# Attention output written token by token, softmax scale moved behind the AV product, chunks transposed at load: a fused attention and two-MoE kernel on one core

## The chip, the cores and the metric

The kernel runs on one core of a Trainium2 chip. The time is device microseconds of one execution; the time before is the median of three runs. Engines are named as in the profile: PE is TensorE (PEld its weight loads), DVE is VectorE, ACT is ScalarE, POOL is GpSimd, and SP is the queue that issues most DMAs.

## The reference

Three layers follow each other. The inputs are drawn at random; all arithmetic is float32.

```python
# attention: B, H, S, D = 8, 8, 576, 64; keys and values are averaged in groups of 8
k_p = k.reshape(B, H, S // 8, 8, D).mean(axis=3)           # 72 keys per head
v_p = v.reshape(B, H, S // 8, 8, D).mean(axis=3)
scores = (1 / np.sqrt(D)) * (q @ k_p^T)
attn = np.exp(scores - max(scores)); attn /= attn.sum(-1, keepdims=True) + 1e-09
x = (attn @ v_p).transpose(0, 2, 1, 3).reshape(4608, 512)   # tokens x (heads, d)
# first MoE (dense): d_model 512, d_ff 1536
g = x @ w_gate
x = (g * sigmoid(g) * (x @ w_val)) @ w_out
# second MoE: 8 experts, top 1, d_ff 1024
logits = x @ w_gate2 + modality_bias[modality_id]; e = argmax(logits)
out = softmax(logits)[e] * (relu(x @ w1[e]) @ w2[e])
```

## The kernel before

**Attention.** The 4608 tokens are worked through in 36 steps of 128 tokens. Two batches make a group of nine steps: a batch has 576 tokens, so four full steps each, and one step (`i == 4`) that takes the last 64 tokens of both. For each batch k is averaged on DVE (`k_pool`, `kp`) and v on POOL (`v_pool`, three adds in a row on `vraw`), and `v_finish` spreads the averaged v into a block-diagonal tile `vb` on POOL. A step runs: `st_scores` (PE writes `sc`, DVE takes the maximum `nm`, ACT makes eight exponentials `e`, one for each head); `st_norm` (DVE sums to `sm`, POOL adds 1e-9, DVE takes the reciprocal, POOL multiplies `e` by it); `st_aT` (PE transposes `e` into `aTp`, DVE or ACT copies it to `at`). `st_av` then works on 256 or 320 tokens at once, for two heads at a time: PE multiplies with `vb` as the stationary operand, so that `xp` has features on partitions and tokens along the row, ACT copies it to `xs`, and the result goes to DRAM already transposed (`xT_d`).

**First MoE.** The tokens are taken in 12 chunks of 384. `x_load` brings a transposed chunk from `xT_d` in four pieces (`xr`) and splits each into a high and a low part (`xh` on ACT, `xl` on DVE) that PE multiplies in its faster float32 form. `gemm1` does 24 matmuls `gv` per chunk and slice of d_ff, `gemm2` nine matmuls `x`. Chunks 0 and 1 run interleaved, because the weights are still being split (`w_split`) then. `x_load(c + 2)` is called after the last `gemm1` of chunk c; `x_load(0)` and `x_load(1)` are called inside the attention. PSUM has eight banks: two of tag `s`, four of tag `x`, two of tag `y`. The output of `gemm2` holds one `y` bank as long as a chunk runs.

**Second MoE.** Routing, then 19 blocks of 256 gathered tokens; `x_trans` transposes each gathered tile on PE (`tp`), and ACT and DVE split it.

**Order.** The attention's pieces are called in the order of keys given by hand (`at_key(x, fn, ...)`, sorted). The build reorders instructions from there and writes one list for each engine; an engine works through its list strictly in order, and so does the SP queue with its DMAs. Where an instruction waits, everything behind it on that engine waits as well.

Of the kernel before, what the change touches and what calls it, by code (L numbers as in the profile page):

```python
# [21 lines left out]
POOL = 8  # L22
# [16 lines left out]

CONST_W = [  # L40
    ("ident", 128), ("vmask", 16), ("idhi", TILES), ("idlo", TILES), ("iota", 128), ("keyw", E), ("le8", E * E),
# [3 lines left out]
def const_array():  # L45
    import numpy as np

    p = np.arange(128)
    parts = {"ident": np.eye(128)}
    vm = np.zeros((128, 4, 2, 2))  # L50
    for r in range(H * KEYS):
        c, row, h = r // 128, r % 128, r // KEYS
        vm[row, h // 2, c - h // 2, h % 2] = 1.0 / 8
    parts["vmask"] = vm.reshape(128, 16)
# [12 lines left out]
def attention_moe_moe2(ctx: ExitStack, tc: tile.TileContext, q, k, v, w_gate, w_val, w_out,  # L67
# [13 lines left out]
    xT_d = [dram.tile([128, 4, 2 * S], F32, name=f"xT{g}") for g in range(4)]  # L81
# [22 lines left out]
    NW1 = 2  # L104
# [71 lines left out]
    def x_load(c):  # L176
        src = xT_d[c // 3]
        c0 = (c % 3) * CH
        hi, lo = [], []
        for k2 in range(2):  # L180
            th = m1.tile([128, 2, CH], F32R, tag="xh", bufs=4, name="xh")
            tl = m1.tile([128, 2, CH], F32R, tag="xl", bufs=4, name="xl")
            for j in range(2):
                raw = m1.tile([128, CH], F32, tag="xr", bufs=2, name="xr")
                sy.dma_start(out=raw, in_=src[:, 2 * k2 + j, c0:c0 + CH])
                ac.copy(th[:, j, :], raw)
                ve.tensor_tensor(out=tl[:, j, :], in0=raw, in1=th[:, j, :].bitcast(F32), op=ALU.subtract)
                hi.append(th[:, j, :])
                lo.append(tl[:, j, :])
        xc[c] = (hi, lo)  # L190
# [3 lines left out]
    with tc.tile_pool(name="p0", bufs=1) as p0:  # L194
# [3 lines left out]
        e_t = [p0.tile([128, 640], F32, name=f"e{i}") for i in range(NE)]  # L198
# [3 lines left out]
        for t in e_t:  # L202
            gp.memset(t[:, 576:640], 0.0)

        k_raw, v_raw, vb_t, q_t, at_t, xs_t, nm_t, sm_t = {}, {}, {}, {}, {}, {}, {}, {}
# [5 lines left out]
        def k_load(b):  # L211
            k_raw[b] = p0.tile([128, 4 * KEYS, POOL], F32, tag="kraw", bufs=2, name="kraw")
            sy.dma_start(out=k_raw[b].rearrange("p k r -> p (k r)"), in_=k[b])

        def v_load(b):
            v_raw[b] = p0.tile([128, 5, POOL, 64], F32, tag="vraw", bufs=2, name="vraw")
            sy.dma_start(out=v_raw[b].rearrange("p c r d -> p (c r d)"), in_=v[b])

        def k_pool(b):
            raw = k_raw.pop(b)  # L220
            kp = p0.tile([128, 4 * KEYS], F32, tag="kp", bufs=2, name="kp")
            ve.tensor_reduce(out=kp, in_=raw, op=ALU.add, axis=AX.X)  # L222
            for w in range(2):
                ps = slice(64 * w, 64 * w + 64)
                ac.activation(out=kb_t[b % 2][ps, :, w, :], in_=kp[ps].rearrange("p (a k) -> p a k", a=4),
                              func=ACTF.Copy, scale=1.0 / 64)

        def v_pool(b):
            t = v_raw.pop(b)
            for w in (4, 2, 1):  # L230
                o = t[:, :, 0:w] if w > 1 else vs_t[b % 2].unsqueeze(2)
                gp.tensor_tensor(out=o, in0=t[:, :, 0:w], in1=t[:, :, w:2 * w], op=ALU.add)  # L232

        def v_finish(b):
            vb = p0.tile([128, 4, 2, 2, 64], F32, tag="vb", bufs=2, name="vb")
            vm = C_["vmask"].rearrange("p (a w r) -> p a w r", a=4, w=2)
            for w in range(2):
                gp.tensor_tensor(out=vb[:, :, w], in0=vs_t[b % 2][:, w:w + 4, :].unsqueeze(2)  # L238
                                 .to_broadcast([128, 4, 2, 64]),
                                 in1=vm[:, :, w].unsqueeze(3).to_broadcast([128, 4, 2, 64]), op=ALU.mult)  # L240
            vb_t[b] = vb.rearrange("p a w r d -> p a w (r d)")
# [36 lines left out]
        def at_tile(b, half):  # L278
            if (b, half) not in at_t:
                at_t[b, half] = p0.tile([128, 5, 256 + 64 * half], F32, tag=f"at{half}", bufs=2, name=f"at{half}")  # L280
            return at_t[b, half]

        def st_aT(x):
            b, i = steps[x]
            e = e_t[x % NE]
            if i < 4:
                views = [(b, i // 2, slice(0, 128), slice(i % 2 * 128, i % 2 * 128 + 128))]
            else:
                views = [(b + w, 1, slice(64 * w, 64 * w + 64), slice(256, 320)) for w in range(2)]
            for c0, cn in ((0, 4), (4, 1)):  # L290
                ap = bank("y", "aTp")[:, 0:cn * 128].rearrange("p (c n) -> p c n", c=cn)
                for c in range(cn):
                    pe.transpose(ap[:, c, :], e[:, (c0 + c) * 128:(c0 + c + 1) * 128], ident)
                for bb, half, ss, cs in views:
                    o = at_tile(bb, half)[:, c0:c0 + cn, cs]
                    if cn == 1 or x % 2:
                        ve.tensor_copy(o, ap[:, :, ss])  # L297
                    else:
                        ac.copy(o, ap[:, :, ss])

        def st_av(b, half, hp):
            n = 256 + 64 * half
            if hp == 0:
                xs_t[b, half] = p0.tile([128, 4, 320], F32, tag="xs", bufs=2, name="xs")
            xs = xs_t[b, half]
            xp = bank("s", "xp")
            for w in range(2):
# [12 lines left out]
        as_, an, av, avs = 3.0, 1.7, 0.7, 0.45  # L320
# [4 lines left out]
        for g in range(4):  # L325
            for b in (2 * g, 2 * g + 1):
                x = 9 * g + (4 if b % 2 else 0) - as_ - 1.0
                at_key(x, k_pool, b)
                at_key(x - 4.0, k_load, b)
                at_key(x - 3.9, q_load, b)  # L330
                x0 = 9 * g + (6 if b % 2 else 1) + av
                at_key(x0 - 1.5, v_finish, b)
                at_key(x0 - 3.0, v_pool, b)
                at_key(x0 - 5.5, v_load, b)
                x1 = 9 * g + (8 if b % 2 else 4) + av
                for hp in range(4):
                    at_key(x0 + hp * avs, st_av, b, 0, hp)
                    at_key(x1 + hp * avs, st_av, b, 1, hp)
        for n in range(3 * NW1 + 4):
            if n < 4:  # L340
                at_key(12.0 + n, w_load, n)
            else:
                at_key(21.0 + (n - 4) * 2.5 + 0.1, w_load, n)
        for n in range(3 * NW1):
            at_key(21.0 + n * 2.5, w_split, n)
        at_key(5.0, load_bias, p0)
# [479 lines left out]
```

## Time and profile before

| | before |
|---|---|
| time, median of 3 runs | 1577.84 us (1576.95 to 1580.01) |
| the profiled execution's own time | 1575.83 us |
| its span in the trace | 1574.1 us |
| first matmul `gv` of the first MoE starts | 192.3 us |
| PE busy, share of the span | 1505.1 us, 96% |
| DVE / ACT / POOL busy | 949.3 / 617.1 / 194.5 us |
| mean granted TensorE clock | 0.983 |

The span runs from the first to the last instruction. A busy share is an average over stages that have different limits: up to 192.3 us no engine is busy all the time, and from there to the end of the first MoE PE is.

### The profile page before, as it was taken

To read this page: it belongs to the slowest core of one execution; us is meant where nothing else is said; L and a number is where in the kernel's file an instruction comes from. 1 tells how busy PE (TensorE), PEld (TensorE's weight loads), DVE (VectorE), ACT (ScalarE), POOL (GpSimd) and SP (SyncE) were. 2 spreads that over 40 slices of the span, in tenths; PEclk is the share of its full clock that TensorE was granted. 3 is DMA by queue.
4 is the path that set the end of the run, shared out by engine and by line. 5 is a ranking of instruction groups with operands and counts; after the bars stand their busy time and mean duration, and the time that the engine had idled before them with its cause. 6 is when DMAs were issued, how large, how long until landed. Compare 5 with 4: busy or idle time off the path is not lost.

```text
span 1574.1 us, 22647 instructions
## 1 busy us (share of the span) xinstructions
PE 1505.1 (96%) x8472; PEld 1367.7 (87%) x8472; DVE 949.3 (60%) x2252; ACT 617.1 (39%) x1385; POOL 194.5 (12%) x201
## 2 busy tenths in 40 slices
PE   5778899999999999999999999999999999999996
PEld 4566699999999999999999999998889889898985
DVE  5677799555555564637272727277986666666660
ACT  4567555432222121212121212123556656666661
POOL 4866300000000000000000000001031111211101
PEclk8998999999999999999999999999999999999998
DMA  7775534210000000000010100007477666666520
GB/s 287 291 268 187 184 139 161 67 31 30 11 30 31 11 31 31 11 30 24 17 41 1 40 1 31 1 21 265 141 231 258 224 229 223 218 225 224 191 98 28
DMA packets 47816, 179.58 MB, mean 114 GB/s; under 512 B 5421, under 2 KB 19921, under 8 KB 34898
## 3 DMA queue, kind: packets, MB, share of 16 engines
q1 hardware_dynamic: 33170, 149.19, 26.9%
q0 software_dynamic: 6080, 19.42, 3.5%
q10 hardware_dynamic: 8448, 9.44, 1.7%
q8 instruction: 68, 1.11, 0.3%
q14 instruction: 50, 0.41, 0.1%
HBM read 149.70 MB, written 28.86 MB: 113 GB/s over the span
## 4 chain that ended last, share of the span: by engine, by line
PE 85%; DVE 4%; issue 4%; POOL 4%; DMA 2%; ACT 1%; POOLq 0%; SPq 0%; ACTq 0%
PE gv L372 38%; PE x L394 19%; PE hp L665 12%; PE po L684 12%; PE xp L308 2%; POOL vraw L232 1%; PE tp L649 1%; POOL e L276 1%; DVE kp L222 1%; DMA x2d<-row 1%; ACT e L267 1%; DVE sm L273 1%; DVE at L297 0%; POOL vb L238 0%; DVE nm L263 0%
## 5 line engine op out<-in xcount | busy, mean ns | idle before, releaser
L372 PE MATMUL gv<-xh,gv 128*128 128x384 f32 x2304 | 611.3, 336 | 0.2 <-DVE t L377 0.2
L372 PEld LDWEIGHTS gv<-xh,gv 128*128 128x128 f32 x2304 | 421.1, 188 | 6.8 <-DVE t L377 0.6
L372 PE MATMUL gv<-xl,gv 128*128 128x384 f32 x1152 | 390.4, 339 | 0.0
L394 PE MATMUL x<-wo,hh 128*128 128x512 f32 x864 | 273.4, 398 | 0.0
L665 PEld LDWEIGHTS hp<-x2hl,w 128*128 128x128 f32 x1824 | 234.1, 189 | 10.9
L665 PE MATMUL hp<-x2hl,w 128*128 128x256 f32 x1824 | 243.1, 282 | 0.0
L372 PEld LDWEIGHTS gv<-xl,gv 128*128 128x128 f32 x1152 | 216.3, 188 | 5.9
L377 DVE SCALAR_TENSOR_TENSOR t<-t,gv 128x384 f32<-128x384 f32 x144 | 79.6, 552 | 233.1 <-ACT t L376 232.6
L376 ACT ACTIVATE t<-gv 128x384 f32<-128x384 f32 x144 | 70.7, 491 | 327.0 <-PE gv L372 326.7
L684 PE MATMUL po<-w,hh 128*128 128x512 f32 x608 | 193.4, 400 | 3.1 <-ACT hh L669 3.1
L414 DVE CUSTOM_DVE_ANT_0 junk<-row,w2g 128x512 bf16<-128x512 f32 x288 | 184.8, 684 | 3.6 <-ACT row L403 3.5
L394 PEld LDWEIGHTS x<-wo,hh 128*128 128x128 f32 x864 | 161.6, 189 | 27.0
L636 DVE TENSOR_TENSOR w<-raw,w 128x512 fp32r<-128x512 f32 x152 | 106.1, 698 | 116.8 <-ACT w L634 116.6
L381 ACT CAST hh<-t 128x384 fp32r<-128x384 f32 x144 | 73.8, 513 | 258.6 <-DVE t L378 258.4
L394 PE MATMUL x<-wo,hl 128*128 128x512 f32 x432 | 171.2, 396 | 0.0
L559 POOL DMA_INDIRECT xg<-x2d,gidx x38 | 38.3, 1007 | 1052.0 <-DVE oidx L546 913.2
L634 ACT CAST w<-raw 128x512 fp32r<-128x512 f32 x152 | 94.0, 619 | 135.4 <-PE po L684 124.8
L378 DVE TENSOR_TENSOR t<-t,gv 128x384 f32<-128x384 f32 x144 | 79.3, 551 | 74.3 <-PE gv L372 74.1
L684 PE MATMUL po<-w,hl 128*128 128x512 f32 x304 | 121.4, 399 | 0.0
L684 PEld LDWEIGHTS po<-w,hh 128*128 128x128 f32 x608 | 103.7, 188 | 17.6 <-ACT hh L669 3.3
L382 DVE TENSOR_TENSOR hl<-t,hh 128x384 fp32r<-128x384 f32 x144 | 80.1, 556 | 51.8 <-ACT hh L381 51.5
L638 DVE TENSOR_TENSOR w<-raw,w 128x512 fp32r<-128x512 f32 x152 | 103.7, 682 | 0.0
(127 smaller groups left out, 1468.8 us busy)
## 6 DMA issues: line engine op xcount, KB each, us to landing
raw<-in_moe_w_dram SPq DMA_DIRECT2D x76, 1024.0 KB, 4.9
vraw<-in_v_dram SPq DMA_DIRECT2D x8, 1280.0 KB, 12.0
x2d<-row SPq DMA_DIRECT2D x36, 256.5 KB, 3.7
kraw<-in_k_dram SPq DMA_DIRECT2D x8, 1152.0 KB, 8.8
qt<-in_q_dram SPq DMA_DIRECT2D x8, 1152.0 KB, 7.0
xr<-xT SPq DMA_DIRECT2D x48, 192.0 KB, 2.4
w2g<-in_moe_w_gate_dram SPq DMA_DIRECT2D x12, 512.0 KB, 3.6
w2g<-in_moe_w_val_dram SPq DMA_DIRECT2D x12, 512.0 KB, 3.5
```

The source lines that it names most:

```text
L372: pe.matmul(p, lhsT=w[:, a, ws], rhs=x[kk], start=n == 0, stop=n == 11)
L377: ve.scalar_tensor_tensor(out=t, in0=t, scalar=1.0, in1=o[0], op0=ALU.add, op1=ALU.mult)
L378: ve.tensor_tensor(out=t, in0=t, in1=o[1], op=ALU.mult)
L381: ac.copy(hh, t)
L382: ve.tensor_tensor(out=hl, in0=t, in1=hh.bitcast(F32), op=ALU.subtract)
L394: pe.matmul(o, lhsT=hx[:, ts], rhs=w[:, f % 2, a, :], start=f == 0 and n == 0, stop=f == NF - 1 and n == 2)
L414: ve.tensor_tensor_reduce(out=junk, in0=r[:, 0:DM], in1=w2g[:, e, :], scale=1.0, scalar=0.0, op0=ALU.mult, op1=ALU.add, accum_out=L[:, tt, ...
L634: ac.copy(h1, src)
L636: ve.tensor_tensor(out=w[:, 1, 0:512].rearrange("p (k f) -> p k f", k=4), in0=src, in1=h1.bitcast(F32), op=ALU.subtract)
L638: ve.tensor_tensor(out=w[:, 1, 512:1024], in0=w2s, in1=w[:, 0, 512:1024].bitcast(F32), op=ALU.subtract)
L665: pe.matmul(hp, lhsT=w[:, a, c0:c0 + 128], rhs=x[:, kk, :], start=n == 0, stop=n == 11)
L684: pe.matmul(b["po"][tt], lhsT=hx[:, ts], rhs=w[:, a, 512:1024], start=f == 0 and n == 0, stop=f == 7 and n == 2)
```

## The change

1. `st_norm` is gone. The exponentials are transposed as they are (`st_aT`), into five blocks of 128 keys (the last has 64) rather than five full ones; the copy of the first four to `at` is on DVE in every third step and on ACT otherwise, and the fifth has its own bank (`aTq`) and its own DVE copy.
2. The sum, the 1e-9 and the reciprocal remain (`st_sum`, `st_rec`), but are used only when the output leaves PSUM: `st_out` multiplies `xp` by the reciprocal on DVE while it evacuates it.
3. `st_av` works on one step. The transposed exponentials are stationary and `vb` is what moves, so that `xp` has 128 tokens on partitions and all 512 features along the row. A matmul of zeros over the whole bank starts the accumulation, and five matmuls of 128, 192, 192, 192 and 64 columns add the key blocks (ten on the step that spans two batches). ACT no longer evacuates `xp`.
4. The result is stored as it is, tokens by features (`x_d`), in 40 DMAs from ACT's queue where there were 16. So `x_load` must transpose: for each of three 128-token tiles and two halves it loads 128 x 256, PE transposes two 128 x 128 blocks into a `y` bank (`xtp`), and ACT and DVE split from there.
5. `vb` has 12 blocks of 64 columns instead of 16. k and v are loaded and averaged in two halves, with two half buffers each. The five weight slots `sr` move to a pool that exists during the attention; six weight pieces are split during the attention as before, at earlier keys.

```diff
-        def st_norm(x):
-            ev = e_t[x % NE][:, 0:576].rearrange("p (h k) -> p h k", k=KEYS)
-            sm = p0.tile([128, 8], F32, tag="sm", bufs=3, name="sm")
-            ve.tensor_reduce(out=sm, in_=ev, op=ALU.add, axis=AX.X)
-            gp.tensor_single_scalar(out=sm, in_=sm, scalar=1e-9, op=ALU.add)
-            ve.reciprocal(out=sm, in_=sm)
-            gp.tensor_tensor(out=ev, in0=ev, in1=sm.unsqueeze(2).to_broadcast([128, 8, KEYS]), op=ALU.mult)
+        def st_sum(x):
+            rc = rc_t[x] = p0.tile([128, 8], F32, tag="sm", bufs=4, name="sm")
+            ve.tensor_reduce(out=rc, in_=e_t[x % NE].rearrange("p (h k) -> p h k", k=KEYS), op=ALU.add, axis=AX.X)
+            gp.tensor_single_scalar(out=rc, in_=rc, scalar=1e-9, op=ALU.add)
+
+        def st_rec(x):
+            ve.reciprocal(out=rc_t[x], in_=rc_t[x])
         def st_aT(x):
...
+            for c in range(4):
+                pe.transpose(ap[:, c, :], e[:, c * 128:(c + 1) * 128], ident)
+            if x % 3 == 0:
+                ve.tensor_copy(at[:, 0:4, :], ap)
+            else:
+                ac.copy(at[:, 0:4, :], ap)
+            ap = bank("y", "aTq")
+            pe.transpose(ap[0:64, 0:128], e[:, 512:576], ident)
+            ve.tensor_copy(at[0:64, 4, :], ap[0:64, 0:128])
...
-            for w in range(2):
-                pe.matmul(xp[:, :n], lhsT=vb_t[b][:, hp, w, :], rhs=at_t[b, half][:, hp + w, :], start=w == 0,
-                          stop=w == 1)
-            ac.copy(xs[:, hp, :n], xp[:, :n])
-            if hp == 3:
-                c0 = (b % 2) * S + half * 256
-                ac.dma_start(out=xT_d[b // 2][:, :, c0:c0 + n], in_=xs[:, :, :n])
+            pe.matmul(xp, lhsT=zero[0:1, 0:128], rhs=zero[0:1, :], start=True, stop=False)
+            for bb, ps in views:
+                for c in range(5):
...
+                    pe.matmul(xp[ps, h0 * 64:(h0 + n) * 64], lhsT=at[ks, c, ps],
+                              rhs=vb_t[bb][ks, i0:i0 + n, :].rearrange("p h d -> p (h d)"),
+                              start=False, stop=c == 4)
+
+        def st_out(x):
+            b, i = steps[x]
+            xn = p0.tile([128, H, D], F32, tag="xn", bufs=3, name="xn")
+            ve.tensor_tensor(out=xn, in0=xp_t.pop(x).rearrange("p (h d) -> p h d", h=H),
+                             in1=rc_t.pop(x).unsqueeze(2).to_broadcast([128, H, D]), op=ALU.mult)
...
     def x_load(c):
...
+        for tt in range(CT):
+            r0 = (c % 3) * CH + tt * 128
+            ts = slice(tt * 128, (tt + 1) * 128)
+            for k2 in range(2):
+                raw = m1.tile([128, 256], F32, tag="xr", bufs=2, name="xr")
+                sy.dma_start(out=raw, in_=src[r0:r0 + 128, k2 * 256:(k2 + 1) * 256])
+                tp = bank("y", "xtp")[:, 0:256].rearrange("p (a n) -> p a n", a=2)
+                for j in range(2):
+                    pe.transpose(tp[:, j, :], raw[:, j * 128:(j + 1) * 128], ident)
+                ac.copy(th[k2][:, :, ts], tp)
+                ve.tensor_tensor(out=tl[k2][:, :, ts], in0=tp, in1=th[k2][:, :, ts].bitcast(F32), op=ALU.subtract)
...
         for x in range(len(steps)):
-            at_key(x - as_, st_scores, x)
-            at_key(x - an, st_norm, x)
-            at_key(x, st_aT, x)
+            at_key(x, st_scores, x)
+            at_key(x + 1.3, st_sum, x)
+            at_key(x + 2.2, st_aT, x)
+            at_key(x + 2.6, st_rec, x)
+            at_key(x + 3.3, st_av, x)
+            at_key(x + 3.6, st_out, x)
```

Three places show how the lists change. In the rows, the tile before the arrow is written, those behind it are read; a number behind an underscore is a buffer.

DVE, some twenty steps into the attention, one step before the change:

```order
L297 COPY at_1074<-aTp 128x128
L263 TENSOR_REDUCE nm<-sc 128x4 x2
L273 TENSOR_REDUCE sm<-e_94 128x8
L297 COPY at_1074<-aTp 128x4x128
L275 RECIPROCAL sm<-sm 128x8
```

And two steps of the changed list:

```order
L273 TENSOR_REDUCE nm<-sc 128x4 x2
L300 COPY at<-aTq 64x128
L282 TENSOR_REDUCE sm<-e_95 128x8
L321 TENSOR_TENSOR xn<-xp,sm 128x512
L286 RECIPROCAL sm<-sm 128x8
L273 TENSOR_REDUCE nm<-sc 128x4 x2
L295 COPY at<-aTp 128x512
L300 COPY at<-aTq 64x128
L282 TENSOR_REDUCE sm<-e_96 128x8
L321 TENSOR_TENSOR xn<-xp,sm 128x512
L286 RECIPROCAL sm<-sm 128x8
```

The multiplication `xn` (of an earlier step) now stands between each sum and its reciprocal, and the reciprocal still comes after POOL's addition of 1e-9 to that sum.

POOL, around one batch's averaging of v, before the change (`vsum` and `vb` are the averaged and the spread v):

```order
L274 TENSOR_SCALAR sm<-sm 128x8
L276 TENSOR_TENSOR e_92<-e_92,sm 128x576
L232 TENSOR_TENSOR vraw<-vraw 128x5x256
L274 TENSOR_SCALAR sm<-sm 128x8
L232 TENSOR_TENSOR vraw<-vraw 128x5x128
L276 TENSOR_TENSOR e_93<-e_93,sm 128x576
L232 TENSOR_TENSOR vsum_88<-vraw 128x320
L274 TENSOR_SCALAR sm<-sm 128x8
L238 TENSOR_TENSOR vb<-vsum_88,cc 128x4x128
```

The same in the changed list, at the longest stretch of work on v:

```order
L283 TENSOR_SCALAR sm<-sm 128x8
L248 TENSOR_TENSOR vb<-vsum_88,cc 128x576
L248 TENSOR_TENSOR vb<-vsum_88,cc 128x64
L240 TENSOR_TENSOR vraw<-vraw 128x3x256
L240 TENSOR_TENSOR vraw<-vraw 128x3x128
L240 TENSOR_TENSOR vsum_89<-vraw 128x192
L240 TENSOR_TENSOR vraw<-vraw 128x2x256
L240 TENSOR_TENSOR vraw<-vraw 128x2x128
L240 TENSOR_TENSOR vsum_89<-vraw 128x128
L283 TENSOR_SCALAR sm<-sm 128x8 x3
```

The multiplications of `e` are gone, and the additions to `sm` stand before or behind whole runs of v work rather than between its pieces.

PE, in the first MoE, where one chunk's `gemm1` follows on the chunk before (`gv` are its matmuls, `x` those of `gemm2`), before the change:

```order
L394 MATMUL x_3285<-wo_2769,hl 128x512
L372 MATMUL gv<-xh,gv_1135 128x384
L372 MATMUL gv<-xl,gv_1135 128x384
L372 MATMUL gv<-xh,gv_1135 128x384 x2
L372 MATMUL gv<-xl,gv_1135 128x384
```

And in the changed list, from behind the first pair of transposes of the chunk after next to the third:

```order
L387 MATMUL gv<-xh,gv_341 128x384
L387 MATMUL gv<-xl,gv_341 128x384
L387 MATMUL gv<-xh,gv_341 128x384 x2
L387 MATMUL gv<-xl,gv_341 128x384
L387 MATMUL gv<-xh,gv_341 128x384
L190 MATMUL xtp<-cc,xr 128x128 x2
L387 MATMUL gv<-xh,gv_341 128x384
L387 MATMUL gv<-xl,gv_341 128x384
L387 MATMUL gv<-xh,gv_341 128x384 x2
L387 MATMUL gv<-xl,gv_341 128x384
L387 MATMUL gv<-xh,gv_341 128x384 x2
L190 MATMUL xtp<-cc,xr 128x128 x2
```

Where the row of `gv` was unbroken, six matmuls stand between the first pair and the second and seven between the second and the third; the other three pairs of the chunk follow at like distances.

## Rows read from the trace of the kernel before

**Rows 1.** Page, part 2: busy tenths and granted clock in 40 slices.

```profile
PE   5778899999999999999999999999999999999996
...
POOL 4866300000000000000000000001031111211101
PEclk8998999999999999999999999999999999999998
```

**Rows 2.** Stretches: length, busy time (instructions) by engine, granted clock, DMA share, GB/s.

```profile
0.00:192.30 192.30, 144.63 (x758) 114.96 (x758) 134.76 (x272) 115.08 (x411) 114.42 (x125) 0.91 0.64 239
192.30:1058.00 865.70, 865.49 (x4540) 808.84 (x4539) 488.51 (x1284) 220.94 (x425) 0.00 (x0) 1.00 0.11 38
```

**Rows 3.** The chain that ended last, attention's start and end, first MoE: start, us.

```profile
6.32 2.56 DVE kp L222
...
184.72 7.99 PE xp L308 x24
...
392.55 4.19 PE gv L372 x24
```

**Rows 4.** Waits of PE and of DVE up to 192.3: total us, times, longest us.

```profile
PE aTp L293 <- POOL e L276: 28.3, 15, 4.4
...
DVE sm L275 <- POOL sm L274: 29.0, 17, 5.2
DVE at L297 <- PE aTp L293: 14.2, 14, 3.1
```

**Rows 5.** Groups on POOL up to 193: busy us, mean ns, idle before.

```profile
L276 POOL TENSOR_TENSOR e<-e,sm 128x576 f32<-128x576 f32 x36 | 42.5, 1180 | 14.6 <-DVE sm L275 8.6 <-DVE at L297 4.3 <-ACT e L267 1.2
L232 POOL TENSOR_TENSOR vraw<-vraw 128x1280 f32<-128x1280 f32 x8 | 23.6, 2955 | 0.0
L238 POOL TENSOR_TENSOR vb<-vsum,cc 128x512 f32<-128x512 f32 x16 | 17.5, 1105 | 5.5 <-PE xp L308 5.1
L232 POOL TENSOR_TENSOR vraw<-vraw 128x640 f32<-128x640 f32 x8 | 12.3, 1537 | 0.6
...
L232 POOL TENSOR_TENSOR vsum<-vraw 128x320 f32<-128x320 f32 x8 | 7.1, 884 | 0.4
```

**Rows 6.** Groups on DVE: copies to at in one row, then by shape.

```profile
L297 DVE COPY at<-aTp 128x128 f32<-128x128 f32 (+3 forms) x60 | 21.9, 382 | 14.2 <-PE aTp L293 14.2
...
L297 DVE COPY at<-aTp 128x512 f32<-128x512 f32 x16 | 11.0, 685 | 7.4 <-PE aTp L293 7.4
...
L297 DVE COPY at<-aTp 128x256 f32<-128x256 f32 x4 | 1.5, 418 | 0.7 <-PE aTp L293 0.7
L297 DVE COPY at<-aTp 128x64 f32<-128x64 f32 x8 | 1.4, 212 | 0.2 <-PE aTp L293 0.2
```

**Rows 7.** Tile x2hl of the second MoE, DVE: ns min/median/max.

```profile
L652 DVE TENSOR_TENSOR x2hl<-tp,x2hl x38: 672/678/692, 1102.4 to 1531.0; 128x512 fp32r<-128x512 f32 x38
```

**Rows 8.** One group on ACT up to 193, copies out of PSUM.

```profile
L310 ACT COPY xs<-xp 128x256 f32<-128x256 f32 x32 | 12.6, 408 | 10.2 <-PE xp L308 10.2
```

**Rows 9.** Timeline of PE in the second MoE: start, length; transposes with and without.

```profile
1242.15 1.57 PE L665 MATMUL hp<-x2hl,w 128*128 128x256 f32 x12
...
1244.96 0.60 PE L649 MATMUL tp<-cc,xg 128*128 128x128 f32 x4
1245.32 1.66 PE L665 MATMUL hp<-x2hl,w 128*128 128x256 f32 x12
...
1251.49 1.57 PE L665 MATMUL hp<-x2hl,w 128*128 128x256 f32 x12
...
1254.31 0.86 PE L665 MATMUL hp<-x2hl,w 128*128 128x256 f32 x6
```

**Rows 10.** Line L649, the transposes: ns min/median/max.

```profile
L649 PE MATMUL tp<-cc,xg x152: 270/272/447, 1100.7 to 1529.8; 128*128 128x128 f32 x152
```

**Rows 11.** The stretch of rows 9 as a window (columns as in rows 2).

```profile
1241.50:1255.00 13.50, 13.50 (x90) 12.13 (x89) 8.12 (x15) 7.58 (x15) 1.96 (x2) 1.00 0.57 200
```

**Rows 12.** Line L185, the loads xr, from 300 to 1000.

```profile
DMA to landing us min/median/max: 2.2/2.4/3.0
```

More of the change, by code (lines that the diff above doesn't have):

```diff
@@ L38 @@
 F32_MAX_HI = 122879.9921875
+VBLK = [(c, h) for c in range(5) for h in range(H) if h * KEYS < (c + 1) * 128 and (h + 1) * KEYS > c * 128]
 CONST_W = [
-    ("ident", 128), ("vmask", 16), ("idhi", TILES), ("idlo", TILES), ("iota", 128), ("keyw", E), ("le8", E * E),
+    ("ident", 128), ("vmask", 12), ("idhi", TILES), ("idlo", TILES), ("iota", 128), ("keyw", E), ("le8", E * E),
 ]
@@ L49, in const_array @@
     parts = {"ident": np.eye(128)}
[L50 to L54, printed above, removed]
+    vm = np.zeros((128, len(VBLK)))
+    for i, (c, h) in enumerate(VBLK):
+        r = c * 128 + p
+        vm[:, i] = (r // KEYS == h) / 8.0
+    parts["vmask"] = vm
     parts["idhi"] = np.tile(np.arange(TILES) * 1.0, (128, 1))
@@ L79, in bank @@
         return psp.tile([128, 512], F32, tag=tag, bufs={"s": 2, "x": 4, "y": 2}[tag], name=name)
-    xT_d = [dram.tile([128, 4, 2 * S], F32, name=f"xT{g}") for g in range(4)]
+    x_d = [dram.tile([2 * S, DM], F32, name=f"xd{g}") for g in range(4)]
     x2_d = dram.tile([NT + 1, DM + 1], F32, name="x2d")
@@ L176, in x_load @@
     def x_load(c):
[L177 to L190, printed above, removed]
+        src = x_d[c // 3]
+        th = [m1.tile([128, 2, CH], F32R, tag="xh", bufs=4, name="xh") for _ in range(2)]
+        tl = [m1.tile([128, 2, CH], F32R, tag="xl", bufs=4, name="xl") for _ in range(2)]
+        for tt in range(CT):
[9 more added lines that the diff above has]
+                ve.tensor_tensor(out=tl[k2][:, :, ts], in0=tp, in1=th[k2][:, :, ts].bitcast(F32), op=ALU.subtract)
+        xc[c] = ([th[i // 2][:, i % 2, :] for i in range(4)], [tl[i // 2][:, i % 2, :] for i in range(4)])
     w2p = [None]
@@ L197, in attention_moe_moe2 @@
         kb_t = [p0.tile([128, 4, 2, KEYS], F32, name=f"kb{i}") for i in range(2)]
-        e_t = [p0.tile([128, 640], F32, name=f"e{i}") for i in range(NE)]
+        kp_t = [p0.tile([128, 4 * KEYS], F32, name=f"kp{i}") for i in range(2)]
+        e_t = [p0.tile([128, H * KEYS], F32, name=f"e{i}") for i in range(NE)]
+        zero = p0.tile([128, 512], BF16, name="zero")
+        ve.memset(zero, 0.0)
         for t in kb_t:
@@ L201, in attention_moe_moe2 @@
             gp.memset(t[64:128, :, 0, :], 0.0)
[L202 to L205 removed]
+        k_raw, v_raw, vb_t, q_t, at_t, xp_t, rc_t = {}, {}, {}, {}, {}, {}, {}
         def q_load(b):
@@ new lines, in k_pool, with v_pool @@
+        def k_pool(b, j):
+            kp = kp_t[b % 2]
+            ve.tensor_reduce(out=kp[:, j * 2 * KEYS:(j + 1) * 2 * KEYS], in_=k_raw.pop((b, j)), op=ALU.add, axis=AX.X)
+            if j:
+                for w in range(2):
+                    ps = slice(64 * w, 64 * w + 64)
+                    ac.activation(out=kb_t[b % 2][ps, :, w, :], in_=kp[ps].rearrange("p (a k) -> p a k", a=4),
+                                  func=ACTF.Copy, scale=1.0 / 64)
+        def v_pool(b, j):
+            t = v_raw.pop((b, j))
+            c0, c1 = VC[j]
@@ L230, in v_pool @@
             for w in (4, 2, 1):
-                o = t[:, :, 0:w] if w > 1 else vs_t[b % 2].unsqueeze(2)
+                o = t[:, :, 0:w] if w > 1 else vs_t[b % 2][:, c0:c1].unsqueeze(2)
                 gp.tensor_tensor(out=o, in0=t[:, :, 0:w], in1=t[:, :, w:2 * w], op=ALU.add)
         def v_finish(b):
[L235 to L240, printed above, removed]
@@ new lines, in st_av @@
+        def st_av(x):
+            b, i = steps[x]
+            at = at_t.pop(x)
+            xp = xp_t[x] = bank("s", "xp")
+            views = [(b, slice(0, 128))] if i < 4 else [(b + w, slice(64 * w, 64 * w + 64)) for w in range(2)]
+            pe.matmul(xp, lhsT=zero[0:1, 0:128], rhs=zero[0:1, :], start=True, stop=False)
+            for bb, ps in views:
+                for c in range(5):
+                    blk_ = [i for i, (cc_, _) in enumerate(VBLK) if cc_ == c]
+                    i0, n = blk_[0], len(blk_)
+                    h0 = VBLK[i0][1]
+                    ks = slice(0, 128 if c < 4 else 64)
+                    pe.matmul(xp[ps, h0 * 64:(h0 + n) * 64], lhsT=at[ks, c, ps],
+                              rhs=vb_t[bb][ks, i0:i0 + n, :].rearrange("p h d -> p (h d)"),
+                              start=False, stop=c == 4)
@@ L286, in st_aT @@
+        def st_out(x):
[3 more added lines that the diff above has]
+                             in1=rc_t.pop(x).unsqueeze(2).to_broadcast([128, H, D]), op=ALU.mult)
+            o = xn.rearrange("p h d -> p (h d)")
             if i < 4:
-                views = [(b, i // 2, slice(0, 128), slice(i % 2 * 128, i % 2 * 128 + 128))]
-            else:
-                views = [(b + w, 1, slice(64 * w, 64 * w + 64), slice(256, 320)) for w in range(2)]
@@ L290, in st_aT @@
[L290 to L307, printed above, removed]
-                pe.matmul(xp[:, :n], lhsT=vb_t[b][:, hp, w, :], rhs=at_t[b, half][:, hp + w, :], start=w == 0,
-                          stop=w == 1)
-            ac.copy(xs[:, hp, :n], xp[:, :n])
-            if hp == 3:
-                c0 = (b % 2) * S + half * 256
-                ac.dma_start(out=xT_d[b // 2][:, :, c0:c0 + n], in_=xs[:, :, :n])
+                r0 = (b % 2) * S + i * 128
@@ L315, in attention_moe_moe2 @@
+                ac.dma_start(out=x_d[b // 2][r0:r0 + 128, :], in_=o)
+            else:
+                for w in range(2):
+                    r0 = w * S + 512
+                    ac.dma_start(out=x_d[b // 2][r0:r0 + 64, :], in_=o[64 * w:64 * w + 64, :])
         ev_ = []
@@ new lines, in attention_moe_moe2 @@
+            at_key(x + 3.3, st_av, x)
+            at_key(x + 3.6, st_out, x)
+        for b in range(B):
+            x = 9 * (b // 2) + (4 if b % 2 else 0)
+            at_key(x - 5.0, k_load, b, 0)
+            at_key(x - 4.9, k_load, b, 1)
+            at_key(x - 4.8, q_load, b)
+            at_key(x - 2.0, k_pool, b, 0)
+            at_key(x - 1.5, k_pool, b, 1)
+            at_key(x - 3.0, v_load, b, 0)
+            at_key(x - 2.9, v_load, b, 1)
+            at_key(x + 0.0, v_pool, b, 0)
+            at_key(x + 0.7, v_pool, b, 1)
+            at_key(x + 1.5, v_finish, b)
@@ L349, in attention_moe_moe2 @@
+        WK = 2.2
+        for n in range(NEARLY + 4):
+            at_key(2.0 + n if n < 4 else 5.0 + (n - 4) * WK + 0.1, w_load, n)
+        for n in range(NEARLY):
+            at_key(5.0 + n * WK, w_split, n)
+        at_key(3.0, load_bias, p0)
+        at_key(30.0, x_load, 0)
+        at_key(34.0, x_load, 1)
         for key, _, fn, args in sorted(ev_, key=lambda t: t[:2]):
             fn(*args)
-        nw = [3 * NW1]
+        nw = [NEARLY]
     w2p[0] = ctx.enter_context(tc.tile_pool(name="w2p", bufs=1, reuse_waits="tile"))
```

79 lines of the change are left out of this document (26 added, 53 removed).

## The prediction

> **What bounds the kernel now.** I read the slices of the page first. PE is full from the sixth slice on, at the full clock; only the first five (about 200 us) are uneven, and POOL works there and hardly afterwards until the last third [rows 1]. Then I cut the span where the first MoE starts. Up to 192.3 us PE is busy for 144.6 us, DVE for 134.8, ACT for 115.1 and POOL for 114.4: nobody is full, so the stage is bound by waits. From 192.3 to 1058 PE is busy for 865.5 of 865.7 us at clock 1.00: anything added to PE there is paid in full [rows 2]. The chain agrees: 24 `gv` matmuls take 4.19 us without a gap, 0.175 us each [rows 3].
>
> Which waits make the attention long? PE waits 28.3 us for POOL's multiplication of `e`. DVE waits 29.0 us for POOL's addition to `sm`, and 14.2 us for transposes that themselves stand behind that multiplication [rows 4]. DVE idles for 192.3 - 134.8 = 57.5 us in all, so 43 of them come from POOL, directly or through PE. POOL is late because it is in order: the multiplications (36 of 1.18 us) share its queue with a batch's v work, whose longest piece takes 2.96 us [rows 5].
>
> So the change does two opposite things. It shortens a stage bound by POOL, and it puts transposes into the stage that PE bounds.
>
> **Attention: what is removed and added.** POOL loses the 42.5 us of multiplications; `vb` shrinks from 16 blocks to 12, from 17.5 to about 13 us. POOL falls from 114 to about 68 us.
>
> DVE loses the copies to `at`, 21.9 us [rows 6]. It gains three things. The scaled evacuation of 128x512 out of PSUM, 36 times: the nearest row reads PSUM and SBUF at the same size and takes 0.678 us [rows 7], so 24.4 us. The copy of 128x512 in every third step: 12 x 0.685 = 8.2. The copy of the fifth block, 36 times: the smallest copies of the old kind take 0.21 us [rows 6], so 7.6. The first two chunks' split costs as many elements as before, and as many weight pieces are split. DVE goes to 134.8 - 21.9 + 24.4 + 8.2 + 7.6 = 153 us and becomes the busiest engine of the stage; halved k loads only divide the same averaging in two.
>
> PE stays where it is. The product with v streamed 64 x 256 + 64 x 320 = 36,864 columns and now streams 40 x 768 = 30,720, plus 36 cheap zero matmuls of 512. ACT loses its copies of `xp` and gains two thirds of those to `at` and 24 DMA issues; it had 77 us to spare. None of that decides.
>
> How much DVE idles now sets the end. It cannot start before the first k lands, at 6.3 us [rows 3]. Below: no other wait, 6.3 + 153 = 159 us. Above: the wait for POOL's `sm` stays at 29 us, 188 us. Between the two I go by the changed order. The reciprocal still waits for POOL, behind the longest stretch of v work: three adds (2.96 + 1.54 + 0.88 = 5.4 us, now in halves) and the large pieces of `vb` (about 1.6), 7.0 us in a row. A step lasts about 4.6 us and `xn` covers 0.7, so one `sm` in each batch comes 1.7 us late: 8 x 1.7 = 14 us. That gives 6.3 + 153 + 14 = 173 us for the end of the attention, **19 us earlier** than 192.3. The old tail, in which PE did nothing but the product with v for 8.0 us [rows 3], goes; the new one finishes the last steps one by one, and I count it as part of DVE's time.
>
> **First MoE: what is added.** Ten of the twelve chunks are transposed under PE's full stage: 10 x 12 = 120 transposes of 128x128. The second MoE does the same operation between the same kind of matmuls. Two groups of four transposes stretch three rounds from 1242.15 to 1251.49, 9.34 us; a round without them, 1251.49 to 1254.31, takes 2.82 us. So 9.34 - 3 x 2.82 = 0.88 us for eight, 0.11 each [rows 9]: 13.2 us for 120. Here they come in pairs, so the switch between the two kinds of matmul is paid twice as often: a group of four delays the next matmul by 0.36 us and makes the next twelve 0.09 longer (1.66 against 1.57), so a pair costs up to 0.18 + 0.09 = 0.27 us and 60 pairs 16.2 us. I take 15.
>
> A record of one transpose lasts 0.272 us [rows 10], but the next starts before it ends, so the sum goes by the spacing and not by the record. The clock doesn't fall for them: it was granted at 1.00 (2.4 GHz) in a window that holds eight transposes among other matmuls [rows 11]. The Trainium skill (TensorE: Matmul & The Clock Gate, section "PE-mode transpose") gives about 275 ns for a transpose in a kernel; by that price 120 of them would cost an estimated 33 us, 18 more than I take. The spacing in this trace disagrees with it, the length of the record agrees.
>
> Then the waits. PE is in order, so a pair whose data or bank isn't there stops the gemm behind it. Data: two buffers `xr`, so the third pair's load starts after the first pair; it lands after 2.4 us [rows 12], while 12 `gv` and one pair fill 12 x 0.175 + 0.27 = 2.4 us. With the hand-overs that is a few tenths late. Bank: one `y` bank is held by the running chunk, so pairs follow each other through one: transposes 0.27 us, ACT's copy of 256 columns 0.41 (the nearest row [rows 8]), DVE's difference 0.42 [rows 6], 1.1 us, against 5 x 0.175 = 0.9 us of `gv` before the second pair and 1.2 before the third. Together about 0.5 us a chunk, **5 us** for ten; below 0, above 0.35 us for each of 60 pairs, 21 us. The stores of the first MoE's output share SP's queue with these loads, but a chunk's stores are due some 20 us after its end and the next chunk's loads only after a whole chunk, 865.7 / 12 = 72 us [rows 2].
>
> **The sum.** Attention -19, transposes +15, waits +5: +1 us on the profiled execution's own 1575.8, about 1576.5. That execution lies 2.0 us under the median of the runs, so I expect a median of about **1578 us**: no change that a measurement of this kernel can tell (0.2%, 3.2 us).
>
> **Rivals.**
> - *DVE keeps its wait and is now the busiest* (slower). DVE's 29 us of waits for POOL stay, because the reciprocal still follows POOL's addition within one instruction. The attention ends at about 188, a gain of 4: 1577.8 - 4 + 20 = 1594. It decides from a gain below 17 us. For it: the changed POOL order has longer runs of v work. Against it: POOL has 46 us less to do. Chance 0.16.
> - *PE waits at every pair* (slower). 60 x 0.35 = 21 us in place of 5: 1594. For it: two buffers and one bank; against it: seven `gv` between most pairs. Chance 0.14.
> - *A transpose costs its record* (slower). 120 x 0.272 [rows 10] = 33 in place of 15: 1596. The spacing in [rows 9] contradicts it, since the next one starts after 0.09 to 0.11. Chance 0.04. (It is the price of the Trainium skill's page named above.)
> - *DVE runs nearly full* (faster). With POOL light, DVE waits hardly: the end is at 162 to 166, a gain of 26 to 30, against 16 to 20 for the transposes: 1564 to 1572. For it: two thirds of DVE's present idle time goes back to POOL. Chance 0.28.
>
> **How the numbers follow.** The central case, 1578, has chance 0.38 and a range of its own from 1570 to 1586. The median before is 1577.8, so "the same" is 1574.7 to 1581.0. I split the central case 0.12 faster, 0.18 the same, 0.08 slower. With the rivals: faster 0.28 + 0.12 = 0.40, same 0.18, slower 0.16 + 0.14 + 0.04 + 0.08 = 0.42. The range runs from the best attention with the cheapest transposes, 1577.8 - 33 + 13 = 1558, to the slow rivals with a little of each other, 1597; less than 2 in 10 lies outside.
>
> **What the profile of the changed kernel would show.** The first `gv` starts near 173 us if the attention's sum holds; DVE is busy for about 153 us before it, and its wait for `sm` is near 14 us. In the first MoE 24 `gv` still take 4.19 us where no pair stands among them, and a chunk takes about 2 us more than before. If PE there waits for `xr` loads or for DVE's `xl`, in total well above 5 us, the waits were undersized. I would be wrong on the good side if DVE's wait for POOL has nearly gone, and on the bad side if it has not shrunk, or if PE turns out to be held by something that I let pass, such as ACT's many DMA issues.

## The result and the profile after

The change made the kernel slower: 1595.28 us median of 3 runs (1593.18 to 1597.96) against 1577.84, a ratio of 1.0109 with a 95% interval from 1.008 to 1.0138. That lies inside the range on record (1558 to 1597), but the forecast of 1578 missed it by 17 us: the attention was to end 19 us earlier and ended 3 us later.

The profiled execution took 1597.96 us, the slowest of the three; the one before was 2.0 us under its median. Its spans, 1595.8 and 1574.1, therefore differ by 21.7 us where the medians differ by 17.4.

The first matmul `gv` starts at 195.6 us (before 192.3). The page's slices of the changed kernel, as in [rows 1]:

```profile
PE   6989999999999999999999999999999999999996
...
POOL 4472000000000000000000000000132111111100
PEclk8899899999999999999999999999999999999998
```

PE stands at 9, 8, 9 and 9 tenths in the second to the fifth slice, where it stood at 7, 7, 8 and 8; POOL, which worked in five slices, works in four. The windows, cut at the first `gv` and where the second MoE begins, with the columns of [rows 2]:

```profile
0.00:195.60 195.60, 169.95 (x961) 135.28 (x961) 147.59 (x309) 101.39 (x360) 77.84 (x117) 0.90 0.66 240
195.60:1118.60 923.00, 920.25 (x4891) 851.72 (x4890) 522.72 (x1377) 234.45 (x469) 1.61 (x2) 1.00 0.13 44
```

In the attention PE is busy for 170.0 us, before for 144.6. Split the end of the attention into PE's busy and idle time: 144.6 + 47.7 before, 170.0 + 25.6 after. The forecast of 173 was worked out from DVE, with PE left at 144.6; that would leave PE 28.4 us of idle time. The idle time came out near that, by chance, since nothing was worked out from it; the busy time did not. What PE, DVE and POOL waited for up to 195.6 (total us, times, longest us):

```profile
PE sc L266 <- DMA qt<-in_q_dram: 10.5, 1, 10.5
PE sc L266 <- ACT e L277: 5.1, 3, 4.2
PE xtp L190 <- DMA xr<-xd: 2.1, 3, 1.1
...
DVE xn L321 <- PE xp L314: 15.1, 13, 2.3
DVE sm L286 <- POOL sm L283: 12.1, 6, 5.2
DVE nm L273 <- PE sc L266: 5.8, 7, 2.9
DVE at L300 <- PE aTq L299: 4.8, 5, 1.6
...
POOL vraw L240 <- DMA vraw<-in_v_dram: 24.1, 5, 10.2
```

PE's 28.3 us of waits for POOL [rows 4] are gone, and DVE's wait for `sm` fell from 29.0 to 12.1. But DVE now waits about 26 us for PE, for the products, the scores and the fifth transpose. And POOL, which stood idle for 0.0 us ahead of its first add of each v [rows 5], now waits 24.1 us for loads of v. What PE does there, by shape (busy us, mean ns, idle before), shortened to the groups that are new or changed:

```profile
L293 PE MATMUL aTp<-cc,e 128*128 128x128 f32 x144 | 26.1, 305 | 1.3 <-DVE at L295 1.1 <-DVE xl L192 0.2
...
L307 PE MATMUL xp<-zero 1*128 1x512 bf16 x36 | 14.5, 408 | 0.0
L299 PE MATMUL aTq<-cc,e 128*64 128x128 f32 x36 | 11.0, 306 | 2.7 <-DVE at L300 1.5 <-ACT at L297 0.7 <-DVE xl L192 0.5
...
L190 PE MATMUL xtp<-cc,xr 128*128 128x128 f32 x24 | 4.5, 284 | 3.1 <-DMA xr<-xd 2.1 <-DVE xl L192 0.9
```

Records overlap, so what one costs PE is read from start to start on its timeline (start, length; a stretch at the full clock):

```profile
60.69 0.60 PE L293 MATMUL aTp<-cc,e 128*128 128x128 f32 x4
61.13 0.27 PE L299 MATMUL aTq<-cc,e 128*64 128x128 f32 x1
61.33 0.39 PE L307 MATMUL xp<-zero 1*128 1x512 bf16 x1
61.65 1.83 PE L314 MATMUL xp<-vb,at 128*128 128x128 f32 x10
63.41 1.25 PE L266 MATMUL sc<-kb,qt 128*128 128x144 f32 x8
```

That is 0.44 us for four transposes, 0.20 for the fifth, 0.32 for the zeros, 1.76 for the product. Summed in this way over every row up to the first `gv`, idle time taken off, PE's busy time goes to (us, worked out from the two timelines):

| PE's work | before | after |
|---|---|---|
| scores | 45.8 | 49.3 |
| transposes of `e` | 24.0 | 27.5 |
| zeros | 0 | 12.3 |
| product with v | 74.9 | 77.2 |
| transposes of chunks 0 and 1 | 0 | 3.7 |
| all, with one small matmul | 144.9 | 170.1 |

The zeros are half of the 25 us. The product streams a sixth fewer columns and takes no less. The scores' matmuls are unchanged; eight take 1.08 us from start to start at the full clock (63.41 to 64.49 on this timeline) where they took 0.99. The one row of eight that follows a transpose in the changed kernel takes 0.99 as well (16.39 to 17.38), those behind the product or the zeros 1.08 or more, so the 0.09 goes with what stands ahead of them.

Both columns also hold time at the lower level of PE's clock (1.2 GHz in place of 2.4). From 30 to 50 us the clock was granted at 0.57, in the kernel before at 0.84; over the whole attention at 0.90 and 0.91. By the two means the lower level cost at most 0.10 x 195.6 us against 0.09 x 192.3, so an estimated 2 of the 25 us may be the clock's and not the work's.

In the first MoE the pairs stand like this (a chunk whose neighbours are all alike):

```profile
735.16 0.38 PE L190 MATMUL xtp<-cc,xr 128*128 128x128 f32 x2
735.29 0.42 PE L387 MATMUL gv<-xh,gv 128*128 128x384 f32 x1
...
736.25 0.34 PE L387 MATMUL gv<-xh,gv 128*128 128x384 f32 x1
736.46 0.44 PE L190 MATMUL xtp<-cc,xr 128*128 128x128 f32 x2
736.65 0.42 PE L387 MATMUL gv<-xh,gv 128*128 128x384 f32 x1
```

The `gv` after a pair starts 0.40 us behind the one ahead of it, where 0.175 is the rule: 0.22 us for the pair at once. The chunk's first pair starts at 735.16, the next chunk's at 812.19: 77.03 us, where 12 rounds of 6.30 (24 `gv` in 4.19, nine `x` in 2.11) made 75.56. That is 1.47 us a chunk, 0.245 a pair. From the first `gv` to the second MoE it is 923.0 us, before 904.8 (192.3 to 1097.1): 18.2 more.

### The profile page after: what moved, and what is told of

Its sections match the earlier page's. It is cut to its first block, busy times and chain, and to the rows that moved or that the text cites. A ratio compares the mean times of both kernels' runs of the same rounds, so it can differ in the third digit from the quotient of the medians.

```text
span 1595.8 us, 23428 instructions
## 1 busy us (share of the span) xinstructions
PE 1544.9 (97%) x8796; PEld 1393.8 (87%) x8796; DVE 965.1 (60%) x2309; ACT 601.9 (38%) x1349; POOL 161.4 (10%) x193
## 4 chain that ended last, share of the span: by engine, by line
PE 86%; DMA 5%; issue 3%; DVE 3%; POOL 2%; ACT 1%; SPq 0%; POOLq 0%; ACTq 0%; DVEq 0%
PE gv L387 37%; PE x L409 19%; PE hp L680 11%; PE po L699 11%; PE xp L314 3%; DMA vraw<-in_v_dram 2%; PE xtp L190 1%; PE sc L266 1%; POOL vraw L240 1%; PE tp L664 1%; PE aTp L293 1%; DMA x2d<-row 1%; DMA xr<-xd 1%; DMA wrow<-in_moe_w_gate_dram 1%; PE xp L307 0%
## 5 line engine op out<-in xcount | busy, mean ns | idle before, releaser
L649 ACT CAST w<-raw 128x512 fp32r<-128x512 f32 x152 | 94.2, 620 | 135.6 <-PE po L699 123.2
```

The source lines that it names most:

```text
L649: ac.copy(h1, src)
```

## Experiments

**The theories.** *PE*: the attention got longer by the work that the change gives PE, the zeros above all, although PE idles elsewhere. *V*: POOL waits 24.1 us for loads of v, and the chain that ended last holds about 33 us of loads of v and 30 of POOL's work on v; by this theory they come late because two loads stand behind blocked ones in SP's queue. *POOL*: the rest of DVE's wait for the addition of 1e-9. Ratios are to the kernel before, run on the same chip between the others (medians there 1576.0 to 1576.5); the ratio of the changed kernel to compare with is 1.0109. The first `gv` of a run is read from one execution, and that of the changed kernel was 2.7 us over its median, so differences of traces can come out larger than those of ratios.

**1. No zeros.** Two lines of `st_av`:

```diff
-            pe.matmul(xp, lhsT=zero[0:1, 0:128], rhs=zero[0:1, :], start=True, stop=False)
-                              start=False, stop=c == 4)
+                              start=True, stop=True)
```

> The changed kernel without the 36 matmuls of zeros; each of the five matmuls of a step overwrites its columns, so the part of the sum that two key blocks share is left out. Theory PE (PE's work sets the end of the attention in the changed kernel: busy 170 of 195.7 us): the 36 matmuls last 14.5 us in the trace, 0.32 us each at the full clock, so the first gv comes 11 to 15 us earlier (181 to 185 us) and the time is 1580 to 1585. Theory V (late loads of v and their averaging on POOL set it): the first gv moves by at most 3 us, 1592 to 1596. Theory POOL (DVE's wait of 12 us for the addition on POOL): at most 3 us too.

1581.80 us, ratio 1.0047 (1.0031 to 1.0063); first `gv` at 182.9, 12.7 us earlier. Its window up to there:

```profile
0.00:182.90 182.90, 151.96 (x925) 128.42 (x925) 150.75 (x309) 101.24 (x360) 76.80 (x117) 0.92 0.70 255
```

PE's busy time fell by 18.0 us and its idle time rose by 5.3. The zeros themselves are 12.3 of the 18.0; the rest is other work that took less time, at a granted clock of 0.92 in place of 0.90. By the ratios the edit is worth 10 us. Theory PE.

**2. No addition of 1e-9.**

```diff
-            gp.tensor_single_scalar(out=rc, in_=rc, scalar=1e-9, op=ALU.add)
```

> The changed kernel without POOL's addition of 1e-9 to the sum (the largest exponential of a row is 1, so in float32 the sum stays what it is). Theory POOL: DVE's 12.1 us of waits for that addition go, first gv near 184 us, 1583. Theory PE: DVE then waits for PE instead (its waits for the products and the scores, 26 us, grow), first gv 0 to 4 us earlier, 1591 to 1596. Theory V: 0 to 3 us.

1588.82 us (nine runs, from 1577.82 to 1595.07), ratio 1.0086 (1.0061 to 1.011). The intervals overlap: a gain of a few us at most, between what theory POOL (1583) and theory PE (1591 to 1596) had said, and nearer to PE. In the trace DVE's 12.1 us of waits are gone, and its waits for the products went from 15.1 to 17.3; the first `gv` is at 190.2, 5.4 us earlier.

**3. v for two batches only.**

```diff
-            at_key(x - 3.0, v_load, b, 0)
...
-            at_key(x + 0.7, v_pool, b, 1)
+            if b < 2:
+                at_key(x - 3.0, v_load, b, 0)
...
+                at_key(x + 0.7, v_pool, b, 1)
```

> The changed kernel with v loaded and averaged for the first two batches only; the other six use the averaged v of those two, so their output is that of other values. DMA loses 12 of 16 loads of v, POOL about 37 of its 78 us. Theory V: the 33 us of loads of v and some 30 us of POOL's work on v that stand in the chain of the attention mostly go; first gv 20 to 30 us earlier (165 to 175 us), 1565 to 1575. Theory PE: PE stays busy for 165 to 170 us, first gv 0 to 8 us earlier, 1587 to 1595. Theory POOL: part of its 12 us, first gv 5 to 12 us earlier.

1584.38 us, ratio 1.0068 (1.0043 to 1.0092), first `gv` at 183.1: between what V and PE had said. POOL's work halves (40.0 us) and PE's busy time falls to 162.5, since less of it runs at the lower clock (granted 0.93 in place of 0.90). So V holds as a second term: 12.5 us in the trace, whose execution was the fastest of the four, and 6.5 by the ratios.

**4. Transposes twice.**

```diff
-                for j in range(2):
+                for j in (0, 1, 0, 1)[0 if c >= 2 else 2:]:
                     pe.transpose(tp[:, j, :], raw[:, j * 128:(j + 1) * 128], ident)
```

> The changed kernel with each transpose of the first MoE's chunks 2 to 11 executed twice in a row (120 more). By the spacing of transposes in the trace before (0.11 us each) 13 us more, first MoE 936 us long in place of 923, 1608. By the length of a transpose's record (0.27 us) 33 us more, 1628. If the pairs were paid as waits (bank, loads) and not as work, less than 5 us more, below 1600.

1606.86 us, ratio 1.0203 (1.0178 to 1.0228). The `gv` of the first MoE now run from 196.3 to 1130.4, 934.1 us; in the changed kernel from 195.6 to 1118.3, 922.7. That is 11.4 us for 120 transposes, 0.095 each; by the ratios it is 15 us, 0.12 each. The record of one in this run:

```profile
L190 PE MATMUL xtp<-cc,xr x264: 270/273/329, 155.5 to 986.3; 128*128 128x128 f32 x132
```

The length 0.273 us is not the price: 33 us are excluded. (The Trainium skill, TensorE: Matmul & The Clock Gate, section "PE-mode transpose", gives about 275 ns for one in a kernel; the length of a record in this run, 0.273 us, agrees with it, and the 0.095 us that PE loses for one does not.)

**5. The zeros put into the kernel before.** In its `st_av` (the tile of zeros is made once, ahead of the attention):

```diff
             xp = bank("s", "xp")
+            pe.matmul(xp[:, :n], lhsT=zero[0:1, 0:128], rhs=zero[0:1, :n], start=True, stop=True)
```

> The kernel before with matmuls of zeros ahead of its products with v: 64 of 256 or 320 columns, 18,432 columns in all, as many as the 36 of 512 that the change adds; they are overwritten at once. Theory PE (PE became the bound only with the change; before, PE was busy for 145 of 192 us and waited for POOL): the zeros fall into PE's waits, first gv at most 5 us later, 1576 to 1581. If PE's work counted fully in the kernel before as well, as taking it out did in the changed one (13 us): 1587 to 1591.

1586.03 us, ratio 1.0066 (1.0049 to 1.0082): 10 us slower, close to the second case (1587 to 1591). The window up to its first `gv`, and PE's longest wait there:

```profile
0.00:201.10 201.10, 162.33 (x821) 116.72 (x822) 141.64 (x273) 114.78 (x411) 115.41 (x125) 0.94 0.62 233
```

```profile
PE aTp L295 <- POOL e L278: 19.1, 7, 4.7
```

PE's busy time rose by 17.7 us, and only 8.9 of them came out of its idle time (47.7 to 38.8; the wait for POOL 28.3 to 19.1). So theory PE has to be put otherwise: it isn't that PE became full by the change. Even where it idled for a quarter of the stage, half of its added busy time was paid. The clock was granted at 0.94 in this window and at 0.91 before, so the added work is rather more than those 17.7 us; how much a higher clock hid is not shown.

**6. No 1e-9 in the kernel before** (the same line of `st_norm` left out).

> The kernel before without POOL's addition of 1e-9 to the sum; the multiplication of the exponentials stays on POOL. DVE's 29.0 us of waits for that addition go. Theory PE: before, the attention hangs on the round trip through POOL, and half of the wait or more comes back: first gv 10 to 25 us earlier (167 to 182 us), 1552 to 1567. Rival: POOL's queue stays as long (POOL busy 114 us, the multiplication waits behind the same work on v), so PE's 28 us of waits for the multiplication only grow: first gv 0 to 5 us earlier, 1572 to 1577.

1571.50 us, ratio 0.9973 (0.996 to 0.9985): 4.5 us, the rival's size. The first `gv` is at 184.3, 8.0 us earlier, in an execution 4 us under the median. DVE's 29.0 us of waits go, PE's wait for the multiplied `e` is still 26.2 us, and DVE waits 29.0 us for the transposes behind it, where it had been 14.2.

**7. The first two chunks loaded earlier.**

```diff
-        at_key(30.0, x_load, 0)
-        at_key(34.0, x_load, 1)
+        at_key(14.0, x_load, 0)
+        at_key(20.0, x_load, 1)
```

> The changed kernel with the loads and transposes of the first two chunks at keys 14 and 20 in place of 30 and 34, where their tokens are already stored. In the chain of the changed kernel the last 40 us of the attention hold two loads of these chunks (2.1 and 2.2 us) with the hand-overs behind them, at a granted clock of 0.86. If PE's waits for these loads count: first gv 4 to 8 us earlier, 1587 to 1591. If only PE's work counts, which stays the same: 0 to 2 us earlier, 1593 to 1596.

1591.64 us, ratio 1.0101 (1.0084 to 1.0118): between the two cases, and not told apart from the changed kernel. In its trace the first `gv` is at 190.9, and from 111 us on the clock is granted at 1.00, but that is one execution.

**8. The same sum without zeros, in eight matmuls.**

```diff
-            pe.matmul(xp, lhsT=zero[0:1, 0:128], rhs=zero[0:1, :], start=True, stop=False)
...
+                    for i0, n in ([(blk_[0], 2)] if c == 0 else [(blk_[0], 1), (blk_[0] + 1, len(blk_) - 1)]):
...
-                              start=False, stop=c == 4)
+                                  start=c == 0, stop=c == 4)
```

> The changed kernel with the same sum, but without the matmuls of zeros: the first matmul of a step starts the bank, and the three blocks that share a head with the block before are cut into a piece that accumulates and a piece that writes first (eight matmuls a step in place of five and one of zeros). Theory PE: 0.32 us a step go at the full clock and three more matmuls of two records each at some 0.03 us of overhead come, 0.17 us; so 36 x 0.15 = 5 us, first gv 4 to 8 us earlier, 1587 to 1591. Theory V: 0 to 2 us, 1593 to 1596.

1594.63 us, ratio 1.0109 (1.0088 to 1.0129): no gain, a miss. PE's busy time up to the first `gv` (198.5) is 170.8 us, as before the edit, but in the slowest of the four executions and at a granted clock of 0.88. So the price is better read at the full clock, from a step's eight matmuls (16 records):

```profile
70.71 2.09 PE L315 MATMUL xp<-vb,at 128*128 128x128 f32 x16
72.73 0.66 PE L293 MATMUL aTp<-cc,e 128*128 128x128 f32 x4
```

That is 2.02 us right behind a transpose. There the five matmuls of the changed kernel take 1.65 (69.94 to 71.59 on its timeline) and the zeros 0.32, together 1.97. Three more matmuls on the same columns cost 0.37 us, as much as the zeros and not the 0.17 expected: the number of narrow matmuls counts, not the columns alone. Five matmuls of which only the first starts the bank were not run.

**9. Loads of weights later.**

```diff
-            at_key(2.0 + n if n < 4 else 5.0 + (n - 4) * WK + 0.1, w_load, n)
+            at_key(2.0 + n if n < 4 else 5.0 + (n - 4) * WK + 2.0, w_load, n)
```

The stall that it aims at, in SP's queue of the changed kernel:

```profile
40.72 0.33 SPq L224 DMA_DIRECT2D vraw<-in_v_dram  x1
55.04 0.33 SPq L126 DMA_DIRECT2D w2g<-in_moe_w_out_dram  x1
55.42 0.90 SPq L217 DMA_DIRECT2D kraw<-in_k_dram  x2
56.42 0.43 SPq L213 DMA_DIRECT2D qt<-in_q_dram  x1
63.80 0.33 SPq L124 DMA_DIRECT2D w2g<-in_moe_w_gate_dram  x1
64.22 0.87 SPq L224 DMA_DIRECT2D vraw<-in_v_dram  x2
```

L126 waits 13.9 us and L124 6.9 for DVE's split, and the loads of k, q and v stand behind.

> The changed kernel with the loads of weight pieces 4 to 9 issued 1.9 steps later, so that SP's queue holds two loads of v ahead of each load of weights that waits for DVE's split (SP waited 36 us for those splits up to 140 us, 13.9 at the longest, with loads of v behind it). If the 11 us that the run without later loads of v gave came from this blocked queue: first gv 5 to 12 us earlier (184 to 190 us), 1583 to 1590. If they came from POOL's averaging or from the transfers themselves: 0 to 3 us, 1592 to 1596.

1592.81 us, ratio 1.011 (1.0094 to 1.0127): the low case. SP's wait for the splits fell from 35.6 to 6.2 us up to 140 us, and the time stayed; the first `gv` of the one trace is at 190.7, 4.9 us earlier. So the blocked queue is at most a small part of the term V; whether it is POOL's averaging, the transfers themselves or the halved buffers that a load waits for stays open (SP waits 18.7 us for POOL's last adds on v in the changed kernel).

**10. Edits 2, 7 and 9 together.**

> The changed kernel with three edits, the output as before: no 1e-9 on POOL, the first two chunks' loads at keys 14 and 20, loads of weight pieces 1.9 steps later. If the stalls are separate, their sum: 6.5 + 3.6 + what the third gives alone (0 to 8), 1577 to 1585. If PE's work alone holds the attention, 1586 to 1592.

1587.98 us, ratio 1.007 (1.0042 to 1.0097): 6 us better than the changed kernel by the ratios, with intervals that overlap. The time is in the range of the case in which PE's work holds, but by their ratios the three edits alone gave 3.6, 1.3 and 0 us, which makes 5; so this run does not tell the two cases apart.

**11. Edits 1 and 3 together.**

> The changed kernel without the zero matmuls and with v loaded and averaged for two batches only (left out: the shared part of the sum, and the other batches' v). Each alone moved the first gv by 12.6 us. If PE's work and the late v are two terms that add: first gv near 170 us, 1570. If either one uncovers the same wait behind it: 178 to 183 us, 1578 to 1582.

1572.17 us, ratio 0.9974 (0.996 to 0.9988); the window up to the first `gv`:

```profile
0.00:173.40 173.40, 147.77 (x926) 125.31 (x926) 143.18 (x309) 100.76 (x360) 38.44 (x81) 0.94 0.63 223
```

The two terms add: 22.2 us of 12.7 + 12.5 in the traces, and by the ratios 21 where 10 and 6.5 alone make 16. PE's busy time is back at 148 us. That the first `gv` comes at 173.4, where the forecast had it, is chance: the forecast kept all of v's work, and this run leaves most of it out.

**12. The kernel before, with edits 6 and 7** (its keys 27 and 30 become 14 and 20).

> The kernel before without POOL's 1e-9 and with the first two chunks' loads at keys 14 and 20, the output as before. The loads carry no transposes here and stand in the chain only with one wait of 3.7 us near the end, so 0 to 3 us better than without the 1e-9 alone: 1568 to 1572, faster than both kernels by 4 to 8 us and by about 25.

1566.67 us, ratio 0.9952 (0.9933 to 0.9971), with the output as before: the best version found, faster than both kernels, though not told apart from experiment 6. The first `gv` is at 187.5, later than there (184.3); in these two traces the gain lies behind it, where the `gv` run for 899.7 us in place of 904.4, and not in the attention as expected. No version with the tokens on partitions and the whole computation beat the kernel before.

## Why the prediction missed

**The step that failed** is "PE stays where it is", with "36 cheap zero matmuls" and "None of that decides". PE's busy time in the attention rose by 25.3 us: zeros 12.3, transposes of `e` 3.5 (the fifth has a bank of its own), scores 3.5, the product 2.3 where 17% fewer columns let me expect less, and 3.7 for the transposes of chunks 0 and 1, which the forecast counted for the other ten chunks only. By the forecast's own columns the product saves 6,144 and the zeros add 18,432; they were put at nothing without a price. That the end of the attention pays for the zeros was shown by taking them out (12.7 us in the trace, 10 by the ratios) and by putting them into the kernel before (10 us).

**A second term was put at nothing.** The forecast has no wait for loads of v, since "halved k loads only divide the same averaging in two" and those of v are not priced. POOL waited for none before and for 24.1 us in the changed kernel; leaving out most of v's loads and averaging gave 12.5 us in the trace and 6.5 by the ratios (experiment 3), on top of the zeros (experiment 11). That run also takes away work which the forecast had counted, so how much of it is the lateness of the loads stays open.

**The rule behind it failed too**: that the busiest engine's sum and its waits give the end. DVE was busy for 147.6 us (forecast 153) and waited 12.1 for `sm` (forecast 14), both near. But it idled for another 36 us, of which the forecast had 6.3 at the start and 26 were waits for PE. Experiment 5 shows that PE's time counted before the change as well, at 75% busy. In this stage each step passes through PE, DVE, ACT and POOL one after another, and each list is in order; I take that as the reason why work on any of them is paid in part, which these runs fit and don't prove. Experiments 2 and 6 say the same of POOL: waits of 12 and 29 us taken away gave a few us.

**POOL** came out at 77.8 us, not 68: adding v in two halves takes 50.0 us where it took 43.0, by the groups. That POOL got light was right, and so was the end of PE's wait for it.

**Prices on DVE.** Two held, `xn` 36 x 0.681 (0.678 taken) and the copies 12 x 0.679 (0.685); the fifth block was dearer, 36 x 0.276 (0.21).

**First MoE**: 18.2 us against 20. Pairs 10 x 1.47 = 14.7 (15 taken); the waits at pairs are 1.0 us where 5 were taken, as PE's list of its waits after the first `gv` shows:

```profile
PE gv L387 <- DVE t L392: 1.7, 1, 1.7
PE xtp L190 <- DMA xr<-xd: 0.8, 2, 0.5
PE xtp L190 <- DVE t L393: 0.2, 1, 0.2
```

**The rivals.** The time is that of the two slow ones, 1594, by neither's way: DVE's wait for POOL did shrink, and PE did not wait at every pair. A transpose at the price of its record fell with experiment 4. The fast rival, an end at 162 to 166, is what POOL's relief alone might have given; not even experiment 11, with most of v's work left out, reached it.

## What to carry to other kernels

- In a stage bound by hand-overs, price what each engine is given, the idle ones too, and check the forecast by busy plus idle time of every engine, not only of the busiest. Here half of 18 us of added busy time on an engine that idled for a quarter of the stage was paid.
- Count matmuls as well as columns, at the starts of a timeline: fewer columns in more and narrower matmuls took as long as before, and a fill with zeros of 0.32 us a step cost 10 us.
- Removing a wait of 29 us gave 4.5 us, because the waits behind it took over. What a wait is worth is what the next one in the loop leaves.

## What the runs showed that I had not expected

- A transpose of 128x128 among the first MoE's matmuls costs PE about 0.1 us (11.4 us for 120 added ones), while its record lasts 0.273.
- A matmul of zeros with one row of 512 columns takes 0.32 us from start to start at the full clock and 0.53 at half of it (the first four of the 36), though its stationary operand has a single partition.
